# Attention and expert layer on one core: denominators transposed out of PSUM by VectorE, and the maxima's transfers issued by SyncE

## The chip, the cores and the metric

The kernel runs on one core of one Trainium2 chip. The time is device microseconds of that core, from runs without the profiler. A separate, profiled execution gave the trace that is read here. Of the engines, TensorE (PE in the rows, PEld for its weight loads) multiplies matrices, VectorE is DVE, ScalarE is ACT, GpSimd is POOL, and SyncE (SP) only issues transfers. "ACTq" and "SPq" are the instruction queues of ScalarE and SyncE, where issues of transfers stand.

## The reference

Pooled attention, then a layer with a squared ReLU, all in float32. There are 4 batches of 8 heads, 1152 keys and 576 pooled queries per head, 64 columns per head; the second layer has 2304 tokens, 512 model columns and 2048 hidden columns.

```python
q_pool = q.reshape(B, H, S // 2, 2, D).mean(axis=3)
scores = scale * np.matmul(q_pool, k.transpose(0, 1, 3, 2))
scores = scores - np.max(scores, axis=-1, keepdims=True)
attn = np.exp(scores)
attn = attn / (np.sum(attn, axis=-1, keepdims=True) + 1e-09)
x = np.matmul(attn, v)            # heads side by side: 2304 x 512
h = x @ w_in
g = s * np.maximum(h, 0.0) ** 2 + b
out = g @ w_out
```

## The kernel before

The attention stage goes through 32 heads, two heads to a pair, in one long loop of steps: nine steps to a head, one for each tile of 128 keys. In step n the kernel multiplies the scores of key tile j of one head into a PSUM tile `s_j` (keys on partitions, queries in two halves of 288 columns, `score_step`, line 486), ScalarE takes their exponential, and three steps later the products of the exponentials with v are added up (`value_step`, lines 518 to 528) in two PSUM tiles `o_0` and `o_1`, one for each half of the queries. Numbers are split into a high and a low part for accuracy: `ph` is the exponential rounded, `pl` the rest, which VectorE or GpSimd computes; one kind of step (`w`) keeps a full `pe` and has no `pl`. There are two `s` buffers. A step's exponentials must be read out before its buffer takes the scores of a later step.

The values have 64 columns, and 64 columns of ones stand beside them. So partitions 0 to 63 of `o` hold the sums of the products and partitions 64 to 127 hold the softmax's denominator, 64 times the same row. When the last product of a head is in, `finish` empties both `o` tiles: ScalarE copies each into `xu` (products) and into `l` (denominators, with 1e-9 added), four copies in all. The next head's first products wait until they are done. When both heads of a pair are there, VectorE transposes `l` in 32x32 blocks into `lt`, takes the reciprocal of one column of each block, and transposes that back over the block; GpSimd multiplies, and SyncE stores the result to DRAM. These steps are put off by the number of ticks in `XT`; one tick is one step of the loop.

The maximum of the scores is subtracted inside the score matmul. A head's maxima are found ahead of its turn, over 27 "units" to a pair: a matmul `m` (line 456) of the same scores with queries on partitions, and a VectorE reduce `pm` (457). After the last unit of a head a short reduce gives `c` (468), 128 partitions by 5 numbers, and two small transfers (471, 472) lay them out as row 64 of `qq`, the moving operand of the score matmul. So the first scores of a head need that head's `c` to have landed. Before the loop 15 steps' worth of units run, which gives the first head its `c`.

Beside this, each pair's keys and queries are loaded two or three pairs ahead (`kraw`, `qraw`; 350, 358), transposed by VectorE (`kT`, `qT`; 411, 413, 415), split, and laid out by transfers into `kk` and `qq` (404 to 407). `qm` is a 64x64 corner of `qT` which ScalarE copies (212).

Every engine and every queue works in the order in which the code issues. There is no scheduler: ticks, `ORD`, `PP`, `PREP` and `XT` fix the order. An instruction that has to wait holds back all that stand behind it on its engine, and an issue of a transfer that has to wait holds back the queue.

When all heads are through, the second layer runs over nine blocks of 256 tokens in three sweeps over the hidden columns. None of the edited lines belongs to it.

Of the kernel before, what the change touches and what calls it, by code (L numbers as in the profile page):

```python
# [8 lines left out]
F32 = mybir.dt.float32  # L9
# [3 lines left out]
AF = mybir.ActivationFunctionType  # L13
ALU = mybir.AluOpType
# [27 lines left out]
XT = (1, 2, 3, 4, 8)  # L42
# [10 lines left out]
def f32(ap):  # L53
    return ap.bitcast(F32)
# [3 lines left out]
def attention_moe_kernel(ctx: ExitStack, tc: tile.TileContext, q, k, v, w_in, w_out, s_in, b_in, out):  # L58
    nc = tc.nc
    B, H, S, D = q.shape  # L60
    SQ = S // 2
    HALF = SQ // 2
    NT, DM = out.shape
    DFF = w_in.shape[1]
    P = 128
    NJ = S // P
    NB = S // 32
    NBQ = SQ // 32
    NT4 = SQ // P
# [6 lines left out]
    EPS = 1e-9  # L76
# [7 lines left out]
    ep = ctx.enter_context(tc.tile_pool(name="ep", bufs=1))  # L84
# [136 lines left out]
    def later(k, fn):  # L221
        step[1] += 1
        queue.append((step[0] + k, step[1], fn))
# [238 lines left out]
    def shift(hd, pm, full, rest):  # L462


        c = ap.tile([P, NT4 + 1], F32R, tag="c", bufs=2, name=f"c{hd}")
        row = qqs[hd % 3][:, 1].rearrange("p a n -> p (a n)")
        h = hd % 2
        nc.vector.tensor_reduce(out=c, in_=pm, axis=AX.X, op=ALU.max)

        def send():  # L470
            nc.scalar.dma_start(f32(row[D:D + 1, :NT4 * P]), f32(c[:, full]))
            nc.scalar.dma_start(f32(row[D:D + 1, NT4 * P:]), f32(c[h * D:(h + 1) * D, rest:rest + 1]))
            holds["c", hd % 3] = hd

        later(1, send)
# [28 lines left out]
    xu = {}  # L504
    inv = {}
    xs = {}

    def value_step(hd, j):
        assert holds["v", hd % 2] == hd
        vv, vl = vvs[hd % 2], vls[hd % 2]  # L510
        ph, pl = prob.pop((hd, j))
        if j == 0:
            acc[hd] = [ps_o.tile([P, 512], F32, tag=f"o{a}", name=f"o{hd}_{a}") for a in range(2)]
        first, last = j == 0, j == NJ - 1
        for a in range(2):
            o = acc[hd][a]
            if pl is None:
                nc.tensor.matmul(o[:, :HALF], vfs[hd % 2][:, j], ph[:, a], start=first, stop=last)  # L518
                if a == 1 and last:
                    finish(hd)  # L520
                for _ in range(3):
                    yield
                continue
            nc.tensor.matmul(o[:, :HALF], vv[:, j], ph[:, a], start=first, stop=False)  # L524
            yield
            nc.tensor.matmul(o[0:D, :HALF], vl[:, j], ph[:, a], start=False, stop=False)  # L526
            yield
            nc.tensor.matmul(o[:, :HALF], vv[:, j], pl[:, a], start=False, stop=last)  # L528
            if a == 1 and last:
                finish(hd)  # L530
            yield

    def finish(hd):
        o = acc.pop(hd)
        p, h = divmod(hd, 2)
        if h == 0:
            xu[p] = (
                ep.tile([P, 2, HALF], F32, tag="xu", name=f"xu{p}"),
                ep.tile([P, 2, HALF], F32, tag="l", name=f"l{p}"),
            )  # L540
        x, l = xu[p]
        r = slice(h * D, (h + 1) * D)
        for a in range(2):
            nc.scalar.activation(x[r, a], o[a][0:D, :HALF], AF.Copy)  # L544
            nc.scalar.activation(l[r, a], o[a][D:P, :HALF], AF.Copy, bias=EPS)  # L545

        def invert():
            lt = ep.tile([P, NBQ, 32], F32, tag="lt", name=f"lt{p}")
            nc.vector.transpose(out=lt, in_=l.rearrange("p a n -> p (a n)"))
            inv[p] = lt  # L550

        def reciprocal():
            lt = inv[p]
            rc = inv[p] = ep.tile([P, NBQ, 1], F32, tag="rc", name=f"rc{p}")
            nc.vector.reciprocal(rc, lt[:, :, 0:1])

        def spread():
            rc = inv[p]
            inv[p] = ep.tile([P, NBQ, 32], F32, tag="lt", name=f"rr{p}")
            nc.vector.transpose(out=inv[p], in_=rc.to_broadcast([P, NBQ, 32]))  # L560

        def scale():
            xo = xs[p] = ep.tile([P, SQ], F32, tag="xo", name=f"xo{p}")
            nc.gpsimd.tensor_tensor(out=xo, in0=x.rearrange("p a n -> p (a n)"), in1=inv.pop(p).rearrange("p j c -> p (j c)"), op=ALU.mult)

        def send():
            nc.sync.dma_start(xd[hd // H][(hd % H) // 2], xs.pop(p))

        if h == 1:
            for at, fn in zip(XT, (invert, reciprocal, spread, scale, send)):  # L570
                later(at, fn)

    load_k(0)
# [47 lines left out]
    for n in range(NS + LAG):  # L621
        hd, j = divmod(n, NJ)

        at = (n - LAG) % NJ if n >= LAG else None
# [16 lines left out]
        if n < NS:  # L641
            p, h = divmod(hd, 2)
# [59 lines left out]
    for m in range(len(work) + DEPTH):  # L702
        if m < len(work):
            i, blk, f, fs = work[m]
# [10 lines left out]
        if m >= DEPTH:  # L715
            _, blk, f, fs = work[m - DEPTH]
# [35 lines left out]
```

## Time and profile before

| | us |
|---|---|
| median of 3 runs | 961.16 (958.78 to 962.41) |
| span of the profiled execution | 960.4 |
| attention stage, to the first matmul of the second layer | 541.9 |
| TensorE busy | 915.8 (95% of the span) |
| VectorE busy | 621.5 (65%) |
| ScalarE busy | 546.4 (57%) |
| GpSimd busy | 507.0 (53%) |

The page gives a span for the profiled execution, from its first to its last instruction, and no other time; the runs without the profiler lie around it. A busy share is an average over stages. A matmul that is late shows as idle time of TensorE before it, with the releaser in square brackets at the end of a row. Starts are in us from the start of the span; the second number of a timeline row is how long the instruction took, in us, and "x2" that two neighbours are shown together.

### The profile page before, as it was taken

How to read it: one execution, taken by the hardware profiler on the slowest of the kernel's cores; microseconds unless marked ns; L12 is line 12 of the kernel's file. 1: busy time of each engine (PE TensorE's matmuls, PEld its weight loads, DVE VectorE, ACT ScalarE, POOL GpSimd, SP SyncE). 2: the span in 40 equal slices, each digit the busy share in tenths (PEclk: the TensorE clock that was granted, in tenths of full speed). 3: DMA queues.
4: the chain of work that ended last, by engine and by line, in shares of the span. 5: the costliest groups of instructions: out<-in, count | busy, mean ns of one | idle time of the engine just before them, and what ended most of it. 6: DMA issues, size and time to landing. Idle time of an engine off the chain costs nothing.

```text
span 960.4 us, 16166 instructions
## 1 busy us (share of the span) xinstructions
PE 915.8 (95%) x5712; PEld 818.2 (85%) x5712; DVE 621.5 (65%) x1168; ACT 546.4 (57%) x1054; POOL 507.0 (53%) x405
## 2 busy tenths in 40 slices
PE   5899999999999999999999989999999999999998
PEld 3788888888888888888888879889999899999997
DVE  5767777777767777877766366767667653334333
ACT  2766666666666676777767656554444433333332
POOL 7567656765676577678756476763453520201000
PEclk9999999999999999999999999999999999999999
DMA  8978776867686778787762245555444432223211
GB/s 151 169 145 171 150 151 122 175 149 148 130 165 145 156 144 187 159 162 147 191 149 69 66 156 187 181 197 163 140 143 165 132 111 67 67 88 107 70 45 44
DMA packets 255312, 131.17 MB, mean 137 GB/s; under 512 B 203776, under 2 KB 227328, under 8 KB 255232
## 3 DMA queue, kind: packets, MB, share of 16 engines
q1 hardware_dynamic: 244512, 129.62, 56.2%
q10 hardware_dynamic: 10720, 0.52, 0.7%
q8 instruction: 46, 0.75, 0.3%
q14 instruction: 34, 0.28, 0.1%
HBM read 68.68 MB, written 18.87 MB: 91 GB/s over the span
## 4 chain that ended last, share of the span: by engine, by line
PE 72%; ACT 13%; DVE 4%; DMA 3%; issue 2%; POOL 2%; ACTq 1%; SPq 0%; POOLq 0%; DVEq 0%
PE h L272 18%; PE y L299 17%; PE s L486 14%; PE o L518 6%; PE m L456 5%; PE o L524 4%; PE o L526 4%; PE o L528 4%; ACT ph L495 4%; ACT xu L544 2%; ACT s L498 2%; ACT l L545 2%; DMA xr<-xd 2%; DVE pm L457 1%; ACT pe L498 1%
## 5 line engine op out<-in xcount | busy, mean ns | idle before, releaser
L457 DVE TENSOR_REDUCE pm<-m 128x1 f32<-128x384 f32 x432 | 230.8, 550 | 98.4 <-PE m L456 92.2
L486 PE MATMUL s<-qq,kk 128*128 128x288 f32 x1152 | 215.6, 309 | 10.6 <-ACT pe L498 6.3
L272 PE MATMUL h<-x,wih 128*128 128x256 f32 x1152 | 213.9, 283 | 6.8 <-DVE gl L286 5.7
L272 PEld LDWEIGHTS h<-x,wih 128*128 128x128 f32 x1152 | 186.8, 189 | 20.9 <-DVE gl L286 6.7
L495 ACT ACTIVATE ph<-s 128x576 fp32r<-128x576 f32 x192 | 125.3, 653 | 130.5 <-PE s L486 108.1
L486 PEld LDWEIGHTS s<-qq,kk 128*128 128x128 f32 x1152 | 173.5, 190 | 26.2 <-ACT pe L498 9.0
L272 PE MATMUL h<-x,wil 128*128 128x256 f32 x576 | 162.8, 283 | 0.0
L501 POOL TENSOR_TENSOR pl<-pe,ph 128x576 fp32r<-128x576 f32 x64 | 91.1, 1424 | 125.7 <-ACT pe L498 115.7
L456 PE MATMUL m<-kh,qz 128*128 128x384 f32 x384 | 155.6, 414 | 1.4 <-DVE pm L457 1.4
L280 DVE SCALAR_TENSOR_TENSOR h<-h,sb,r 128x256 f32<-128x256 f32 x144 | 70.3, 488 | 114.7 <-ACT r L289 114.7
L253 POOL TENSOR_TENSOR x<-xr,x 128x1024 fp32r<-128x1024 f32 x27 | 64.9, 2402 | 148.8 <-ACT x L212 143.1
L524 PE MATMUL o<-ph,vv 128*128 128x288 f32 x384 | 119.1, 310 | 9.0 <-issue 5.3
L518 PE MATMUL o<-pe,vf 128*128 128x288 f32 x384 | 123.2, 405 | 0.0
L501 DVE TENSOR_TENSOR pl<-s,ph 128x576 fp32r<-128x576 f32 x128 | 96.4, 753 | 37.6 <-ACT s L498 32.6
L289 ACT ACTIVATE r<-h 128x256 f32<-128x256 f32 x144 | 55.8, 387 | 112.1 <-PE h L272 112.1
L526 PE MATMUL o<-ph,vl 128*64 128x288 f32 x384 | 113.3, 295 | 0.0
L299 PE MATMUL y<-wol,gh 128*128 128x512 f32 x288 | 113.3, 393 | 0.0
L299 PE MATMUL y<-woh,gl 128*128 128x512 f32 x288 | 113.0, 392 | 0.0
L299 PE MATMUL y<-woh,gh 128*128 128x512 f32 x288 | 112.9, 392 | 0.0
L528 PE MATMUL o<-pl,vv 128*128 128x288 f32 x384 | 112.8, 294 | 0.0
L272 PEld LDWEIGHTS h<-x,wil 128*128 128x128 f32 x576 | 110.1, 191 | 0.0
L283 ACT ACTIVATE gh<-h,sb 128x256 fp32r<-128x256 f32 x144 | 68.3, 474 | 64.4 <-DVE h L280 64.1
(89 smaller groups left out, 1500.5 us busy)
## 6 DMA issues: line engine op xcount, KB each, us to landing
kk<-kh SPq DMA_DIRECT2D x32, 576.0 KB, 6.0
kraw<-in_k_dram SPq DMA_DIRECT2D x64, 144.0 KB, 3.5
vf<-in_v_dram SPq DMA_DIRECT2D x32, 288.0 KB, 4.4
kk<-kT SPq DMA_DIRECT2D x32, 288.0 KB, 4.9
qq<-qh SPq DMA_DIRECT2D x64, 144.0 KB, 6.0
xr<-xd SPq DMA_DIRECT2D x18, 512.0 KB, 3.9
qraw<-in_q_dram SPq DMA_DIRECT2D x122, 72.0 KB, 2.6
wsti<-in_moe_w_in_dram SPq DMA_DIRECT2D x16, 512.0 KB, 4.7
```

Of the source, the lines that this page charges most:

```text
L272: nc.tensor.matmul(h[:, :TB], st[:, c, :], mv[:, c, :], start=(n == 0), stop=(n == 3 * NC - 1))
L280: nc.vector.scalar_tensor_tensor(out=t, in0=h[:, :TB], scalar=sb[:, 0:1], in1=r, op0=ALU.mult, op1=ALU.mult)
L299: nc.tensor.matmul(y[:, :DM], st[:, ts_], mv, start=(first and n == 0), stop=(last and n == 2))
L456: nc.tensor.matmul(ps[:, :KB], st, khs[p][:, e * KB:(e + 1) * KB], start=True, stop=True)
L457: nc.vector.tensor_reduce(out=pms[p][:, col, e:e + 1], in_=ps[:, :KB], axis=AX.X, op=ALU.max)
L486: nc.tensor.matmul(ps[:, a, :HALF], kk[:, i, j * P:(j + 1) * P], qq[:, i, a], start=(i == 0), stop=(i == 1))
L495: nc.scalar.activation(ph, ps[:, :, :HALF], AF.Exp, scale=SCALE)
L501: fresh.append(lambda: eng.tensor_tensor(out=pl, in0=full, in1=f32(ph), op=ALU.subtract))
L518: nc.tensor.matmul(o[:, :HALF], vfs[hd % 2][:, j], ph[:, a], start=first, stop=last)
L524: nc.tensor.matmul(o[:, :HALF], vv[:, j], ph[:, a], start=first, stop=False)
L526: nc.tensor.matmul(o[0:D, :HALF], vl[:, j], ph[:, a], start=False, stop=False)
L528: nc.tensor.matmul(o[:, :HALF], vv[:, j], pl[:, a], start=False, stop=last)
```

## The change

Two things change. In `finish`, ScalarE keeps the copy of the products, and VectorE transposes the denominators out of PSUM straight into `lt`, one 64x288 transpose for each `o` tile and head. The 1e-9 is added afterwards to the one column of each block that is used (`guard`), the reciprocal is taken in place, and the spread result has a buffer of its own. In `shift`, the two small transfers of `c` are issued by SyncE instead of ScalarE.

```diff
         def send():
-            nc.scalar.dma_start(f32(row[D:D + 1, :NT4 * P]), f32(c[:, full]))
-            nc.scalar.dma_start(f32(row[D:D + 1, NT4 * P:]), f32(c[h * D:(h + 1) * D, rest:rest + 1]))
+            nc.sync.dma_start(f32(row[D:D + 1, :NT4 * P]), f32(c[:, full]))
+            nc.sync.dma_start(f32(row[D:D + 1, NT4 * P:]), f32(c[h * D:(h + 1) * D, rest:rest + 1]))
@@ finish
-                ep.tile([P, 2, HALF], F32, tag="l", name=f"l{p}"),
+                ep.tile([P, NBQ, 32], F32, tag="lt", name=f"lt{p}"),
...
             nc.scalar.activation(x[r, a], o[a][0:D, :HALF], AF.Copy)
-            nc.scalar.activation(l[r, a], o[a][D:P, :HALF], AF.Copy, bias=EPS)
-
-        def invert():
-            lt = ep.tile([P, NBQ, 32], F32, tag="lt", name=f"lt{p}")
-            nc.vector.transpose(out=lt, in_=l.rearrange("p a n -> p (a n)"))
-            inv[p] = lt
+            nc.vector.transpose(out=lt[r].rearrange("p j c -> p (j c)")[:, a * HALF:(a + 1) * HALF], in_=o[a][D:P, :HALF])
+
+        def guard():
+            rc = inv[p] = ep.tile([P, NBQ, 1], F32, tag="rc", name=f"rc{p}")
+            nc.vector.tensor_scalar(out=rc, in0=lt[:, :, 0:1], scalar1=1.0, scalar2=EPS, op0=ALU.mult, op1=ALU.add)
 
         def reciprocal():
-            lt = inv[p]
-            rc = inv[p] = ep.tile([P, NBQ, 1], F32, tag="rc", name=f"rc{p}")
-            nc.vector.reciprocal(rc, lt[:, :, 0:1])
+            nc.vector.reciprocal(inv[p], inv[p])
 
         def spread():
             rc = inv[p]
-            inv[p] = ep.tile([P, NBQ, 32], F32, tag="lt", name=f"rr{p}")
+            inv[p] = ep.tile([P, NBQ, 32], F32, tag="rr", name=f"rr{p}")
```

VectorE's order at the end of head 8, the first of pair 4, before. `pl_2` belongs to step 2 of the next head, `kT` and `qT` to the preparation of a later pair:

```order
L457 TENSOR_REDUCE pm_1988<-m_12_2162 128x1
L501 TENSOR_TENSOR pl_2_2158<-s_2_2152,ph_2_2157 128x576
L413 STREAM_TRANSPOSE kT_2125<-kraw_1842 128x576
L457 TENSOR_REDUCE pm_1988<-m_13_2185 128x1
L457 TENSOR_REDUCE pm_1988<-m_14_2191 128x1
L468 TENSOR_REDUCE c_2194<-pm_1988 128x5
L415 STREAM_TRANSPOSE qT_2126<-qs_2127 128x576
```

And the same place now:

```order
L457 TENSOR_REDUCE pm_1985<-m_12_2158 128x1
L545 STREAM_TRANSPOSE lt_2163<-o_0_1989 64x288
L545 STREAM_TRANSPOSE lt_2163<-o_1_1990 64x288
L501 TENSOR_TENSOR pl_2_2154<-s_2_2148,ph_2_2153 128x576
L413 STREAM_TRANSPOSE kT_2121<-kraw_1839 128x576
L457 TENSOR_REDUCE pm_1985<-m_13_2181 128x1
L457 TENSOR_REDUCE pm_1985<-m_14_2187 128x1
L468 TENSOR_REDUCE c_2190<-pm_1985 128x5
L415 STREAM_TRANSPOSE qT_2122<-qs_2123 128x576
```

The two transposes stand between the reduce and `pl_2`, and `c` and `qT` come after them. Each of the two waits for ScalarE's copy of the same `o` tile.

ScalarE's order at the same place, before:

```order
L544 ACTIVATE xu_2166<-o_0_1992 64x288
L545 ACTIVATE l_2167<-o_0_1992 64x288
L544 ACTIVATE xu_2166<-o_1_1993 64x288
L545 ACTIVATE l_2167<-o_1_1993 64x288
L495 ACTIVATE ph_3_2181<-s_3_2175 128x576
L498 ACTIVATE pe_3_2180<-s_3_2175 128x576
L471 DMA qq_98<-c_2194 1x128x4
L472 DMA qq_98<-c_2194 1x64x1
L495 ACTIVATE ph_4_2213<-s_4_2208 128x576
L498 ACTIVATE s_4_2208<-s_4_2208 128x2x288
L212 ACTIVATE qm<-qT_2126 64x64 x2
L490 ACTIVATE pe_5_2238<-s_5_2233 128x576
```

And now:

```order
L544 ACTIVATE xu_2162<-o_0_1989 64x288
L544 ACTIVATE xu_2162<-o_1_1990 64x288
L495 ACTIVATE ph_3_2177<-s_3_2171 128x576
L498 ACTIVATE pe_3_2176<-s_3_2171 128x576
L495 ACTIVATE ph_4_2209<-s_4_2204 128x576
L498 ACTIVATE s_4_2204<-s_4_2204 128x2x288
L212 ACTIVATE qm<-qT_2122 64x64 x2
L490 ACTIVATE pe_5_2234<-s_5_2229 128x576
```

Two copies and two issues are gone; `qm` still stands in front of `pe_5`.

SyncE's order at the start of the program now; `c_232` holds the maxima of head 0, and `kk_95`, `qq_98` are the operands of head 1:

```order
L358 DMA qraw_160<-in_q_dram 32x18x32 x8
L404 DMA kk_95<-kT_132 64x1152
L404 DMA kk_95<-kh_135 64x2x1152
L405 DMA qq_98<-qh_136 64x576
L406 DMA qq_98<-qh_136 64x576
L407 DMA qq_98<-qT_133 64x576
L471 DMA qq_97<-c_232 1x128x4
L472 DMA qq_97<-c_232 1x64x1
L363 DMA vf_104<-in_v_dram 128x9x64
```

Before, the two `c_232` rows were not on this queue; they stood on ScalarE, behind the preparation of pair 0 and in front of the first exponential. The other rows are as they were.

## Rows read from the trace of the kernel before

**Rows 1.** The page: the chain that ended last, by engine.
```profile
PE 72%; ACT 13%; DVE 4%; DMA 3%; issue 2%; POOL 2%; ACTq 1%; SPq 0%; POOLq 0%; DVEq 0%
```

**Rows 2.** Windows: length, then busy us of PE, PEld, DVE, ACT, POOL; clock; DMA.
```profile
200.00:300.00 100.00, 96.72 (x610) 86.72 (x609) 72.65 (x133) 67.38 (x124) 66.02 (x54) 1.00 0.75 151
```

**Rows 3.** Waits, 60 to 500 us: total us, times, longest.
```profile
PE s L486 <- ACT pe L498: 5.0, 9, 0.6
```

**Rows 4.** Timeline of ScalarE, end of head 8: start, took, instruction, idle before.
```profile
174.90 0.41 ACT L545 ACTIVATE l<-o 64x288 f32<-64x288 f32 x1
...
176.19 0.65 ACT L495 ACTIVATE ph<-s 128x576 fp32r<-128x576 f32 x1
...
177.78 0.80 ACTq L472 DMA_DIRECT2D qq<-c  x1
178.63 0.65 ACT L495 ACTIVATE ph<-s 128x576 fp32r<-128x576 f32 x1 [1.25 <-PE s L486]
...
179.85 0.53 ACT L212 ACTIVATE qm<-qT 64x64 fp32r<-64x64 f32 x2
180.40 0.66 ACT L490 ACTIVATE pe<-s 128x576 f32<-128x576 f32 x1
```

**Rows 5.** Timeline of VectorE, the same place.
```profile
174.61 0.76 DVE L501 TENSOR_TENSOR pl<-s,ph 128x576 fp32r<-128x576 f32 x1
...
176.99 0.17 DVE L468 TENSOR_REDUCE c<-pm 128x5 fp32r<-128x15 f32 x1
177.08 0.77 DVE L415 STREAM_TRANSPOSE qT<-qs 128x576 f32<-128x576 f32 x1
```

**Rows 6.** Timeline of TensorE: scores of steps 4, 6, and the next head's first.
```profile
177.43 0.80 PE L486 MATMUL s<-qq,kk 128*128 128x288 f32 x4 [0.56 <-ACT pe L498]
...
180.87 0.69 PE L486 MATMUL s<-qq,kk 128*128 128x288 f32 x4
...
185.50 0.91 PE L486 MATMUL s<-qq,kk 128*128 128x288 f32 x4
```

**Rows 7.** Groups by line, VectorE: busy us, mean ns | idle before, releaser.
```profile
L457 DVE TENSOR_REDUCE pm<-m 128x1 f32<-128x384 f32 x432 | 230.8, 550 | 98.4 <-PE m L456 92.2
...
L549 DVE STREAM_TRANSPOSE lt<-l 128x576 f32<-128x576 f32 x16 | 12.4, 774 | 7.2 <-ACT l L545 7.2
...
L555 DVE RECIPROCAL rc<-lt 128x18 f32<-128x18 f32 x16 | 4.0, 247 | 0.1
```

**Rows 8.** Timeline after an odd head, number 17: ScalarE's `ph_3`, step 4's scores.
```profile
321.65 0.66 ACT L495 ACTIVATE ph<-s 128x576 fp32r<-128x576 f32 x1 [0.41 <-issue]
...
321.79 0.69 PE L486 MATMUL s<-qq,kk 128*128 128x288 f32 x4
```

**Rows 9.** Timeline of SyncE's queue at the start.
```profile
18.80 6.45 SPq L358 DMA_DIRECT2D qraw<-in_q_dram  x8
...
29.89 0.92 SPq L407 DMA_DIRECT2D qq<-qT  x1
```

**Rows 10.** Timeline at the start: the second c transfer, and the first scores.
```profile
20.32 0.60 ACTq L472 DMA_DIRECT2D qq<-c  x1
...
22.02 1.33 PE L486 MATMUL s<-qq,kk 128*128 128x288 f32 x4 [0.24 <-DVE pm L457]
```

**Rows 11.** Transfers (KB each, us to landing) and SyncE's waits, at the start.
```profile
qq<-c ACTq DMA_DIRECT2D x1, 0.2 KB, 1.8
...
sb<-in_moe_s_dram SPq DMA_DIRECT2D x1, 0.5 KB, 3.8
...
SPq L358 <- DMA qq<-c: 2.3, 1, 2.3
```

**Rows 12.** Timeline after head 28: a long issue, and scores that wait.
```profile
500.93 2.65 ACTq L472 DMA_DIRECT2D qq<-c  x1
...
505.44 0.79 PE L486 MATMUL s<-qq,kk 128*128 128x288 f32 x4 [1.61 <-ACT pe L490]
```

**Rows 13.** Windows in the second layer's start; the clock is the third from last.
```profile
574.00:575.00 1.00, 1.00 (x6) 1.00 (x6) 0.90 (x2) 0.00 (x0) 1.00 (x1) 0.50 0.00 0
```

More of the change, by code (lines that the diff above doesn't have):

```diff
@@ L538, in finish @@
                 ep.tile([P, 2, HALF], F32, tag="xu", name=f"xu{p}"),
-                ep.tile([P, 2, HALF], F32, tag="l", name=f"l{p}"),
+                ep.tile([P, NBQ, 32], F32, tag="lt", name=f"lt{p}"),
             )
-        x, l = xu[p]
+        x, lt = xu[p]
         r = slice(h * D, (h + 1) * D)
@@ L569, in finish @@
         if h == 1:
-            for at, fn in zip(XT, (invert, reciprocal, spread, scale, send)):
+            for at, fn in zip(XT, (guard, reciprocal, spread, scale, send)):
                 later(at, fn)
```

## The prediction

> **What bounds the kernel now.** The chain that ended last is 72% TensorE and 13% ScalarE [rows 1], so I read the attention stage, which holds every edited line, by windows first. From 200 to 300 us TensorE is busy 96.7 of 100 us, VectorE 72.7 and ScalarE 67.4, with the granted clock at 1.00 [rows 2]: time is to be had only where TensorE stands still. The MoE stage runs no edited line after its first microseconds, so only its start time can move.
>
> The table of waits names the place. Between 60 and 500 us score matmuls wait for ScalarE's `pe` exponential, 5.0 us in 9 waits [rows 3]. The timeline around one of them, 174 us, shows why: a head has just finished, ScalarE copies its two accumulators out in four copies, and the exponentials of the next step stand behind them [rows 4]. I call a head with an even number boundary A, one with an odd number boundary B. There are 16 of each. At A the chain is xu, l, xu, l, then `ph_3` at 176.19, `pe_3` behind it, then the score matmuls of step 4 at 177.43, which name `pe` as what they waited for [rows 4, 6]. The two `qq<-c` issues follow on ScalarE's queue until 178.58 and hold back `ph_4`, which starts after 1.25 us of idleness [rows 4]. At B the step-4 scores start at 321.79 and wait for no `pe` [rows 8].
>
> **The change, part by part.**
>
> *ScalarE at A.* Each head loses two l copies. The first l starts at 174.90 where the second xu can now start, the second xu takes about as long as an l, 0.41, and 0.04 is the gap behind it [rows 4]: `ph_3` starts at 175.35 instead of 176.19, so 0.84 us earlier. `pe_3` follows it as before, and step 4 starts at 176.59 instead of 177.43, if nothing else is late. The next accumulators are no obstacle: they wait for two VectorE transposes, priced next, that end at 175.43 and 175.90, and TensorE has the max matmuls and three products of the first accumulator between.
>
> *VectorE at A.* Two 64x288 transposes out of PSUM are added, for which the trace has no row. The 128x576 transpose from SBUF takes 774 ns, that is 0.17 beside 1 column per 1.04 ns; the PSUM reduce over 384 columns takes 550 ns, 0.15 beside the same rate [rows 7]. So I take 300 + 175 = 0.475 us for 288 columns. From below, 0.17 us (the same fixed part and hidden columns) and from above 0.77 us (the whole 576-column transpose [rows 7]) bound it. In the order each transpose stands behind ScalarE's xu of the same accumulator. VectorE is free when `pl_2` began, at 174.61 [rows 5], and the first xu ends at about 174.90, so the first transpose runs from 174.95 to 175.43, the second to 175.90. Behind them in VectorE's order stand `pl_2` itself, a `kT` transpose, two reduces, c and the `qT` transpose that ended at 177.85 [rows 5]. All keep their 3.24 us and slide by 1.29: `qT` ends at 179.14.
>
> What is late next is ScalarE's `qm`, which reads `qT`: 179.18 to 179.71 (0.53), then `pe_5` (0.66) until 180.39 [rows 4]. The scores of step 6 now wait for `pe_5` (their buffer has changed), so they start at 180.45. Before, they started at 180.87 [rows 6]. So of 0.84 gained, 0.42 remains at A: 16 x 0.42 = 6.7 us.
>
> [...]
>
> *The issues leave ScalarE.* At a usual A they delay `ph_4` by about 1 us, and that is already inside the 0.42, since `ph_4` is no longer the limit. Where an issue is slow it costs more: at 500.93 one took 2.65 us and the scores at 505.44 waited 1.61 us for it [rows 12]. That wait goes: 1.6 us. So A gains 6.7 + 1.6 = 8.3 us.
>
> *At B* the second reduce and `pl_2` move behind the transposes, and step 4 now waits for `pe_3`. From A's spacing (175.35 to 176.59 for `ph_3` to step 4) and B's `ph_3`, which at 321.65 stood behind two copies and 0.41 us of issuing and can now start at about 320.4, step 4 starts at about 321.7, against 321.79 [rows 8]: nothing, between a gain of 0.1 and a loss of 0.3 per B. The 16 guards, the reciprocals in place and the shorter transposes run in VectorE's idle time, which is 27% of the stage [rows 2]. They hide there; uncovered they cost 16 x 0.25 = 4 us at most (the price of a reciprocal [rows 7]). The later multiply and store have no reader before the MoE.
>
> *The transfers on SyncE's queue.* In the middle of the stage there is room. At A, c slides with `qT`, from 176.99 to 178.28 [rows 5]; with issues of about 0.6 us the second starts at 179.0, and 3.8 us later (the landing used below) it is there, at 182.8. The next head's first scores start at 185.50, or 0.42 earlier [rows 6]. At the start there is none. The first maxima were issued by ScalarE at 20.32 (the second of two transfers) and landed 1.8 us later, at 22.1; the first scores began at 22.02, and their last of four matmuls, about 0.72 us later, needed them [rows 10, 11]. In the new order the two transfers stand on SyncE behind eight `qraw` loads and the five `kk` and `qq` transfers of head 1, which SyncE issued from 18.80 to 30.81 [rows 9]. One wait in that run goes away, the 2.3 us for c itself [rows 11], so the run ends at 28.5. The two issues start at 28.5 and 29.1. A half-kilobyte transfer on SyncE's queue at 31.75 took 3.8 us to land [rows 11], so c is there at 32.9 instead of being in time for a matmul at 22.74. The start is 10.2 us later; 0.3 us of waiting for a `qraw` load behind it goes. Cost: 9.9 us. Bounds: 8.2 with the landing of 1.8 us, 12.5 if the 2.3 us remain. Nothing hides it, as every engine's program passes through the first scores. The pause may lower the granted clock: in the second layer it stood at 0.50 between 574 and 575 [rows 13], shortly after a pause. At half speed three such microseconds would cost an estimated 1.5 us more; I add nothing, since the first four score matmuls took 1.33 us before as well [rows 10], against 0.69 later [rows 6].
>
> **The sum.** 960.4 + 9.9 - 8.3 = 962.0 us of span. The median of the runs, 961.16, is 0.8 above the profiled span; so 962.8, call it 963.
>
> **The rivals.** *ScalarE's relief is kept whole.* If the transposes are near the lower bound and `qT` is not late, 0.84 remains at each A: 16 x 0.84 + 1.6 = 15.0 us, so 960.4 + 9.9 - 15.0 + 0.8 = 956 us. For it speaks that ScalarE's chain is what ends the wait now [rows 3]; against it, that VectorE has no pause in its order between 174 and 177.9 [rows 5].
>
> *The first maxima are not late*, because SyncE gets through its earlier transfers sooner: 960.4 - 8.3 + 0.8 = 953 us. Against it: the order, and the five issues behind the loads, which alone took 5.5 us, from 25.25 to 30.81 [rows 9].
>
> *Slower: VectorE's order gives everything back.* Its place is A, `pl_2` to `qT` to `qm` to `pe_5`. It decides from the point where VectorE's slide is 1.29 + 0.42 = 1.71 us, that is with transposes of about 0.69 us each. Then the steady gain is nothing: 960.4 + 9.9 + 0.8 = 971 us. For it: 0.69 lies inside my bound of 0.77. Against: both nearest rows give 0.475.
>
> *Slower: SyncE's queue makes c late at later heads too*, since it holds waits of its own; 1 us late at 16 heads gives 963 + 16 = 979 us. The change does do what it says: the order shows both moves.
>
> **How the numbers follow.** The forecast has 0.56, with 958 to 968 of its own; relief kept whole 0.14, no late start 0.06, VectorE gives back 0.17, later heads late 0.07. The range from 955 to 970 takes in the first two and the better part of the fourth. A difference under 0.5%, 4.8 us, cannot be told from no change here. Faster: 0.06 and 0.08 of the second case, 0.14. Slower: 0.17, 0.07 and 0.04 of the forecast's upper end, 0.28. Same: 0.58.
>
> **What would show it.** Right: the first `ph` at about 33.5 us instead of 23.4; transposes near 0.475 us; at A, step 4 waiting for `pe_3` some 0.8 us earlier, step 6 waiting for `pe_5`, about 0.4 us earlier; the MoE starting 1 to 2 us later than at 541.9. Wrong: c landed before 25 us; `qT` done before 178.5 in its place; waits of first scores for `qq<-c` at later heads.

## The result, and the profile after

The changed kernel takes 966.55 us (median of four runs, 965.36 to 967.24), beside 961.11 for the kernel before: ratio 1.0053, 95% interval 1.0035 to 1.0072. That lies in the range, 3.6 us above the forecast. The prediction took a difference under 0.5% as no change; this one, 0.53%, lies at that line. The profiled execution has a span of 965.5 us, 5.0 more than before.

The best single view is the start of every step's first score matmul, in both traces. The differences of neighbouring starts, summed by place, say where the time went (us; minus is faster). Pairs count from 0; B of pair n is the boundary at which pair n begins, so [rows 8] shows B of pair 9, and A of pair n lies between its two heads:

| | forecast | measured |
|---|---|---|
| start, to step 8 of the first head | +9.9 | +10.3 |
| A, sixteen times | -8.3 | -9.3 |
| B of pairs 1 to 9 | 0 | +1.1 |
| B of pairs 10 to 15 | 0 | +5.5 |
| elsewhere in the attention stage | 0 | -0.2 |
| attention stage | +1.6 | +7.4 |
| MoE | 0 | -2.4 |
| span | +1.6 | +5.0 |

*The start.* SyncE's issues (start, duration, queue, line; the last two are c) and TensorE's first scores:

```profile
18.72 4.62 SPq L358 DMA_DIRECT2D qraw<-in_q_dram  x8
...
28.19 0.82 SPq L407 DMA_DIRECT2D qq<-qT  x1
29.11 0.54 SPq L471 DMA_DIRECT2D qq<-c  x1
29.70 0.65 SPq L472 DMA_DIRECT2D qq<-c  x1
```

```profile
22.28 0.61 PE L486 MATMUL s<-qq,kk 128*128 128x288 f32 x1 [0.24 <-DVE pm L457]
31.82 1.06 PE L486 MATMUL s<-qq,kk 128*128 128x288 f32 x3 [8.94 <-issue]
```

The first of four matmuls ran on time. The second needs c (row 64 of `qq`, in the code), and it and the two behind it came 8.94 us later; the prediction had only the last of the four need it. The releaser is printed as "issue", which here hides a landing: the row of the queue names it, the second issue at 29.70 with 2.2 us to its landing. [rows 10] showed the four together in 1.33 us.

*A, the end of head 8, the place of [rows 4 to 6].* ScalarE, VectorE, and the scores of steps 4, 5 and 6:

```profile
182.89 0.68 ACT L544 ACTIVATE xu<-o 64x288 f32<-64x288 f32 x2
183.46 0.64 ACT L495 ACTIVATE ph<-s 128x576 fp32r<-128x576 f32 x1
184.00 0.65 ACT L498 ACTIVATE pe<-s 128x576 f32<-128x576 f32 x1
185.72 0.65 ACT L495 ACTIVATE ph<-s 128x576 fp32r<-128x576 f32 x1 [1.08 <-PE s L486]
...
187.51 0.52 ACT L212 ACTIVATE qm<-qT 64x64 fp32r<-64x64 f32 x2 [0.60 <-DVE qT L415]
188.06 0.66 ACT L490 ACTIVATE pe<-s 128x576 f32<-128x576 f32 x1
```

```profile
183.31 0.86 DVE L545 STREAM_TRANSPOSE lt<-o 64x288 f32<-64x288 f32 x2 [0.32 <-ACT xu L544]
184.20 0.76 DVE L501 TENSOR_TENSOR pl<-s,ph 128x576 fp32r<-128x576 f32 x1
184.88 0.77 DVE L413 STREAM_TRANSPOSE kT<-kraw 128x576 f32<-128x576 f32 x1
...
186.59 0.17 DVE L468 TENSOR_REDUCE c<-pm 128x5 fp32r<-128x15 f32 x1
186.70 0.78 DVE L415 STREAM_TRANSPOSE qT<-qs 128x576 f32<-128x576 f32 x1
```

```profile
185.00 0.69 PE L486 MATMUL s<-qq,kk 128*128 128x288 f32 x4
186.69 0.92 PE L486 MATMUL s<-qq,kk 128*128 128x288 f32 x4
188.77 0.80 PE L486 MATMUL s<-qq,kk 128*128 128x288 f32 x4
```

From step 3, step 4 comes 0.83 us earlier than before, step 5 0.69, step 6 0.50, step 7 0.40. Not every A is like this one, as is told further down. The end of the give-back is readable: `qm` waits 0.60 us for `qT`, `pe` follows, and the next scores start 0.05 us after it.

*B, which was to cost nothing.* At pair 9, [rows 8] of before; VectorE, GpSimd and TensorE:

```profile
327.79 0.75 DVE L501 TENSOR_TENSOR pl<-s,ph 128x576 fp32r<-128x576 f32 x1
328.46 0.78 DVE L549 TENSOR_SCALAR rc<-lt 128x18 f32<-128x18 f32 x1
329.15 0.55 DVE L457 TENSOR_REDUCE pm<-m 128x1 f32<-128x384 f32 x1
```

```profile
327.78 1.42 POOL L501 TENSOR_TENSOR pl<-pe,ph 128x576 fp32r<-128x576 f32 x1 [3.31 <-ACT pe L498]
```

```profile
327.75 0.81 PE L486 MATMUL s<-qq,kk 128*128 128x288 f32 x4
...
329.75 0.44 PE L456 MATMUL m<-kh,qm 128*128 128x384 f32 x1
330.03 0.69 PE L486 MATMUL s<-qq,kk 128*128 128x288 f32 x4
```

The guard works on 18 numbers per partition and takes 0.78 us. It ends at 329.24, GpSimd's `pl` at 329.20. The reduce behind it is late, so the max matmul (its buffer) and the scores are late: step 4 to 5 takes 2.28 us instead of 1.85. Before, step 4 began at 321.79 [rows 8] and step 5 here:

```profile
323.64 0.69 PE L486 MATMUL s<-qq,kk 128*128 128x288 f32 x4
```

The whole line of the guard (count, shortest, median, longest in ns):

```profile
L549 DVE TENSOR_SCALAR rc<-lt x16: 164/774/1409, 74.5 to 550.7; 128x18 f32<-128x18 f32 x16
```

From pair 10 on the conversion of the second layer's weights stands there as well. Pair 11:

```profile
392.82 1.65 DVE L161 TENSOR_SCALAR wabo<-whmo 128x512 int32<-128x512 int32 x1
394.38 0.16 DVE L549 TENSOR_SCALAR rc<-lt 128x18 f32<-128x18 f32 x1
```

```profile
392.77 1.41 POOL L501 TENSOR_TENSOR pl<-pe,ph 128x576 fp32r<-128x576 f32 x1
```

```profile
395.07 0.45 PE L456 MATMUL m<-kh,qm 128*128 128x384 f32 x1 [1.02 <-DVE pm L457]
```

Here `wab` is caught instead, 1.65 us, and the guard behind it runs free in 0.16. In pairs 12 to 14 `wab` gets in first (0.42) and the guard is caught for 1.38. Before, the line of `wab` took this (two tiles, `wi` and `wo`):

```profile
L161 DVE TENSOR_SCALAR wabi<-whmi x3: 416/786/860, 353.4 to 483.1; 128x512 int32<-128x512 int32 x3
L161 DVE TENSOR_SCALAR wabo<-whmo x3: 821/842/2323, 385.8 to 517.0; 128x512 int32<-128x512 int32 x3
```

So one instruction with durations of 0.42, of 0.79 to 0.86 and of 2.32 us stood in the trace of before: the sign that something else decides how long it lasts.

*The MoE* lasts 416.1 us instead of 418.5. The difference opens at one place. Before, TensorE waits 1.80 us for VectorE's `gl` there, and the stretch at half clock of [rows 13] follows (0.50); after, the same wait is 0.44 and no such stretch follows (the clock is 1.00 from 577.4 to 587.4):

```profile
573.13 0.61 PE L272 MATMUL h<-x,wih 128*128 128x256 f32 x2 [1.80 <-DVE gl L286]
```

```profile
579.47 0.51 PE L272 MATMUL h<-x,wih 128*128 128x256 f32 x2 [0.44 <-DVE gl L286]
```

About 1.4 us are the shorter wait and another 1.4 the full clock of the matmuls behind it; 0.4 came back elsewhere. In the traces of the experiments the MoE lasts 415.8 to 417.3. That the change shortened the wait is not shown: with the transfers alone from the third head on it is 2.41 us, and no half clock follows it (the mean granted clock of that profiled run is 1.000).

### The profile page after: what moved, and what is told of

Read it like the earlier page. It is cut to its first block, busy times and chain, and to the rows that moved or that the text cites. A ratio compares the mean times of both kernels' runs of the same rounds, so it can differ in the third digit from the quotient of the medians.

```text
span 965.5 us, 16055 instructions
## 1 busy us (share of the span) xinstructions
PE 916.7 (95%) x5712; PEld 816.3 (85%) x5712; DVE 646.9 (67%) x1232; ACT 517.1 (54%) x990; POOL 507.8 (53%) x405
## 4 chain that ended last, share of the span: by engine, by line
PE 73%; DVE 10%; ACT 7%; DMA 4%; issue 2%; POOL 1%; SPq 1%; ACTq 0%; POOLq 0%; DVEq 0%
PE h L272 18%; PE y L299 17%; PE s L486 13%; PE m L456 6%; PE o L518 5%; PE o L524 5%; PE o L526 5%; PE o L528 5%; DVE pm L457 2%; ACT ph L495 2%; DVE lt L545 2%; ACT s L498 2%; DMA wsto<-in_moe_w_out_dram 2%; DVE pl L501 1%; ACT xu L544 1%
## 5 line engine op out<-in xcount | busy, mean ns | idle before, releaser
L524 PE MATMUL o<-ph,vv 128*128 128x288 f32 x384 | 116.1, 302 | 10.8 <-DVE lt L545 10.8
```

## The experiments

The kernel before was timed again beside each group of experiments, with medians of 960.07 to 961.11 us, so medians of different groups compare to about 1 us. The ratios are to the kernel before in the same group.

**The transposes alone.**

```diff
-            nc.sync.dma_start(f32(row[D:D + 1, :NT4 * P]), f32(c[:, full]))
+            nc.scalar.dma_start(f32(row[D:D + 1, :NT4 * P]), f32(c[:, full]))
```

(and the second transfer likewise)

> The change without its second half: VectorE transposes the denominators, but c still leaves on ScalarE's queue. Theory (the halves are coupled: the two transposes put c about 1 to 2 us later on VectorE, and the issues of c stand on ScalarE in front of ph_3 at B and of ph_4 at A): the start is as before, no 10 us; at each B ph_3 starts some 1.9 us later and step 4, which now waits for pe_3, about 3 us; at each A step 6 is about 1.3 us later than before. 960 + 16 x (3.0 + 1.3) = about 1030 us. Rival (the start's delay is all that separates the change from its gain, and c's issue hides): 966.5 - 10.3 = about 956 us.

989.23 us, ratio 1.0312 (1.0291 to 1.0333). ScalarE at A:

```profile
182.90 0.65 ACT L498 ACTIVATE pe<-s 128x576 f32<-128x576 f32 x1
185.69 0.49 ACTq L471 DMA_DIRECT2D qq<-c  x1
186.28 0.56 ACTq L472 DMA_DIRECT2D qq<-c  x1
186.88 0.65 ACT L495 ACTIVATE ph<-s 128x576 fp32r<-128x576 f32 x1 [3.34 <-PE m L456]
```

The issue waits for c, which VectorE now has later, and the next `ph` stands behind it for 3.34 us. The start is as before; against before most A's lose 0.6 to 1.1 us and most B's 0.8 to 1.3. The coupling is shown; I had priced B three times too high. One thing more shows in this run. The guard stands at the same place, right behind `pl_2`, and takes 0.17 us at B of every pair from 1 to 15, where the changed kernel has 0.77 to 1.41 in most; its longest is at the end of the last head. GpSimd's `pl` of B of pair 9, held back with ScalarE's `pe`, starts only after it:

```profile
L549 DVE TENSOR_SCALAR rc<-lt x16: 165/168/509, 66.0 to 572.1; 128x18 f32<-128x18 f32 x16
```

```profile
337.82 0.17 DVE L549 TENSOR_SCALAR rc<-lt 128x18 f32<-128x18 f32 x1
```

```profile
340.12 1.44 POOL L501 TENSOR_TENSOR pl<-pe,ph 128x576 fp32r<-128x576 f32 x1 [7.66 <-ACT pe L498]
```

**The transfers alone**, in the kernel before.

> The change without its first half: the l copies stay on ScalarE, c leaves on SyncE's queue. Theory: the start costs the same 10.3 us as in the changed kernel; at A TensorE already ran without a pause from step 4 to step 7, so only the A's with a slow issue gain, 1.6 to 5 us in all: 961.1 + 10.3 - (1.6 to 5) = 966 to 970 us. Rival (SyncE's queue costs nothing or the extra time of the changed kernel comes from the transposes): 958 to 961 us.

964.18 us, ratio 1.0044 (1.0030 to 1.0058), just under what was expected. The start costs +9.8. But A of pairs 0 to 9 gains 0.83 or more with all four copies still on ScalarE, which neither theory had, and step 1 to 2 of 14 pairs loses 0.70 (one of them 0.56). The scores of step 4 and ScalarE's `pe` of step 3:

```profile
185.22 0.56 PE L486 MATMUL s<-qq,kk 128*128 128x288 f32 x3
```

```profile
185.23 0.65 ACT L498 ACTIVATE pe<-s 128x576 f32<-128x576 f32 x1
```

Step 4 starts while `pe_3` has just begun: it uses the other `s` buffer. In this kernel's code step 4 at A waits for VectorE's `pl_2`; in the kernel before it waits for ScalarE at A of pairs 0 to 9, and for `pl_2` from pair 10 on. Most of what is gained there (14.8 us at A) is lost at pair starts (9.6), where products now wait for GpSimd's `pl` (6.1 us in 14 waits).

**Only the first head's c from ScalarE**, in the changed kernel.

```diff
-            nc.sync.dma_start(f32(row[D:D + 1, :NT4 * P]), f32(c[:, full]))
+            eng = nc.scalar if hd == 0 else nc.sync
+            eng.dma_start(f32(row[D:D + 1, :NT4 * P]), f32(c[:, full]))
```

(and the second transfer likewise)

> The changed kernel, but the very first head's c is issued by ScalarE as before, all 31 others by SyncE. Theory (the start's cost is the first head's c behind SyncE's loads, once): the first three score matmuls no longer pause 8.9 us, first ph near 23.5, 966.5 - 10 = about 956.5 us. Rival (a later c or the pause's after-effects carry part of it): 960 to 963 us.

962.79 us, ratio to the kernel before 1.0028 (1.0017 to 1.0039): the rival. SyncE, and the second head's first scores (lines from 471 on stand one further down in this kernel):

```profile
32.97 3.65 SPq L350 DMA_DIRECT2D kraw<-in_k_dram  x4
36.72 5.11 SPq L358 DMA_DIRECT2D qraw<-in_q_dram  x8
41.94 0.53 SPq L472 DMA_DIRECT2D qq<-c  x1
```

```profile
44.03 0.72 PE L487 MATMUL s<-qq,kk 128*128 128x288 f32 x3 [3.54 <-DMA qq<-c]
```

Ten microseconds earlier, the second head needs its c while SyncE is still issuing twelve loads: 5.4 us come back there. In the changed kernel the late start had hidden this.

**The first two heads' c from ScalarE** (`hd < 2` in the line above).

> The changed kernel, the c of the first two heads issued by ScalarE, the other 30 by SyncE. Theory (with only the first there, the second head's c stood behind the twelve key and query loads on SyncE, 3.5 us of waiting and two slow steps, 5.4 us in all; with both there the whole start cost is back): 966.5 - 10.3 = about 956.5 us. Rival (the third head's c is late in its turn, or ScalarE is held by the second c): 959 to 963 us.

957.00 us, ratio 0.9954 (0.9941 to 0.9967). The first head is 10.4 us shorter and nothing else differs by 0.1 us.

**No guard.** 1e-9 is left out.

```diff
-            nc.vector.tensor_scalar(out=rc, in0=lt[:, :, 0:1], scalar1=1.0, scalar2=EPS, op0=ALU.mult, op1=ALU.add)
...
-            nc.vector.reciprocal(inv[p], inv[p])
+            nc.vector.reciprocal(rc, lt[:, :, 0:1])
```

> The changed kernel without the guard: 1e-9 is left out, the reciprocal reads the transposed column directly. Theory (the guard, 18 elements per partition, is held until GpSimd's pl ends, 0.77 to 1.4 us instead of 0.16, and holds up a reduce and with it a max matmul at B): step 4 to 5 at B back from 2.28 to about 1.85 us in pairs 1 to 9, about 1.2 us back in each of pairs 12 to 14, pairs 10 and 11 little, since there another VectorE operation is held; in all 4 + 4 = 8 us: about 958.5 us. Rival (B's loss comes from the reduces having slid behind the transposes, and the guard is 0.16 us each): -1.6 us at most, 965 us.

961.15 us, 5.4 below the changed kernel. B of pairs 1 to 9 gains 0.33 each, B of pairs 11 and 15 1.2 to 1.3 each, and pairs 12 to 14 only 0.1, against an expected 1.2, since now `wab` is caught there. VectorE and GpSimd of pair 12:

```profile
420.97 1.64 DVE L161 TENSOR_SCALAR wabi<-whmi 128x512 int32<-128x512 int32 x1
```

```profile
420.92 1.40 POOL L501 TENSOR_TENSOR pl<-pe,ph 128x576 fp32r<-128x576 f32 x1
```

**The guard as another kind of instruction**, same place, same operands; 1e-9 is left out.

```diff
-            nc.vector.tensor_scalar(out=rc, in0=lt[:, :, 0:1], scalar1=1.0, scalar2=EPS, op0=ALU.mult, op1=ALU.add)
+            nc.vector.tensor_reduce(out=rc, in_=lt[:, :, 0:1], axis=AX.X, op=ALU.max)
```

> The changed kernel, the guard at its old place, but as a reduce over one element (1e-9 is left out; same input, output and 18 elements per partition) instead of a multiply-add. Theory (this form of instruction, reading and writing SBUF, is what GpSimd's pl holds; a reduce is not held): it lasts about 0.2 us, step 4 to 5 at B about 1.95 us, the same time as without a guard: 961 to 962 us. Rival (whatever stands there is held, by a semaphore or by its place): 0.77 us again in pairs 0 to 8, 965 to 967 us.

961.54 us, as without a guard. The line now:

```profile
L549 DVE TENSOR_REDUCE rc<-lt x16: 170/173/185, 73.8 to 544.6; 128x18 f32<-128x18 f32 x16
```

It runs in 0.17 us right beside GpSimd's `pl`. So it was neither a semaphore nor the place, but the kind of instruction, at a time when `pl` runs.

**The guard directly behind the transposes.**

```diff
         if h == 1:
-            for at, fn in zip(XT, (guard, reciprocal, spread, scale, send)):
+            guard()
+            for at, fn in zip(XT[1:], (reciprocal, spread, scale, send)):
```

> The changed kernel, the guard issued directly behind the two transposes of an odd head instead of one tick later. Theory (the guard was held by GpSimd's pl; earlier, GpSimd works on nothing that holds it): the guard takes 0.16 us in pairs 0 to 9, step 4 to 5 at B falls from 2.28 to about 1.95 us, the saving is that of leaving the guard out less up to 0.1 us a head: 966.5 - 5.4 + (0 to 1.6) = 961 to 962.7 us. Rival (the cost is that of one more VectorE instruction at B, wherever it stands): 965 to 967 us.

963.59 us, 3.0 below the changed kernel and 0.9 above the end of what was expected:

```profile
L549 DVE TENSOR_SCALAR rc<-lt x16: 176/179/2171, 72.0 to 546.6; 128x18 f32<-128x18 f32 x16
```

The guard is free now, but `wab` is caught for 1.43 us in pairs 11 to 14 in its stead, and in pair 15 the guard lasts 2.17 us beside a 2.4 us GpSimd operation.

**`qm` behind `pe_5`.**

```diff
-PREP = (..., ("qm", 13), ...)
+PREP = (..., ("qm", 14), ...)
```

> The changed kernel, qm issued one tick later, behind pe_5 instead of in front of it. Theory (at A VectorE's later qT holds qm and so pe_5 and the scores of step 6): step 5 to 6 at A falls from 2.07 to about 1.88 us and step 6 to 7 from 1.60 to 1.50, 0.2 to 0.3 us at 14 heads: 962.5 to 964 us. Rival (step 6 waits for something else): 966 to 967 us.

963.17 us. Step 5 to 6 at A falls by 0.15 to 0.20 and step 6 to 7 by 0.10, at 14 heads. That `qm`, late with `qT`, takes back part of the gain at A is shown.

**All together.** Besides three edits from above (the first two c from ScalarE, the early guard, `qm` behind `pe_5`), `wab` of the weight conversion comes two ticks later, at the tick of `wA`, which takes 0.68 us there in the changed kernel.

```diff
-STA = (0, 1, 3, 5, 7, 18, 19, 20)
+STA = (0, 1, 5, 5, 7, 18, 19, 20)
```

> All three at once, and besides the two steps of the weight conversion that stand on VectorE at B of pairs 10 to 15 (wab and wA) one after the other at the later of their ticks, when GpSimd has nothing that holds them. Theory (the savings add up, and the held conversion cost about 1.1 us in four to five pairs): 966.5 - 10 - 5 - 3 - 4.5 = about 944 us. Rival (each stall gone uncovers the next one, half is kept): 953 to 956 us.

948.70 us, ratio 0.9864 (0.9848 to 0.9880): faster than both kernels. Against the changed kernel the first head gives 10.1 us, B of pairs 1 to 9 0.3 each, B of pairs 10 to 14 3.1 in all, A 0.3 each at 14 heads. Three things kept it from 944: VectorE has both conversion steps at one place (+0.5 us at step 6 to 7 of five pairs), pair 15's guard is caught again (2.17 us), and the MoE lasts 1.0 us longer, for which no cause is shown.

**`wA` one tick later** (`STA = (0, 1, 5, 6, ...)`).

> The combined kernel with wA one tick behind wab instead of together with it. Theory (in pairs 10 to 14 both at one place made VectorE late by 0.5 us at step 6 to 7): 5 x 0.5 = 2.5 us less, 946.2 us. Rival (wA then meets GpSimd's xo and is held): 948.7 us or more.

950.71 us: the rival. `wA`, 1.69 us here and 0.68 in the changed kernel, and the GpSimd operation beside it:

```profile
413.72 1.69 DVE L164 SCALAR_TENSOR_TENSOR wAi<-wsti,wabi 128x512 int32<-128x512 int32 x1
```

```profile
413.43 1.42 POOL L562 TENSOR_TENSOR xo<-xu,rr 128x576 f32<-128x576 f32 x1 [2.13 <-DVE rr L558]
```

**The transfers alone, from the third head on**, in the kernel before.

> The kernel before, with c on SyncE's queue from the third head on, the first two heads' c by ScalarE as before; nothing else changed. Theory (the start cost comes off whole, as it did with the transposes): 964.2 - 9.9 = about 954.3 us, which is less than the 957.0 us of the same with the transposes, so the transposes as changed cost 2.7 us. Rival (the gain at the ends of heads comes from the transposes and ScalarE's two copies): 958 to 961 us.

954.32 us, ratio 0.9928 (0.9910 to 0.9946). With the same start the transposes make it 957.00: as changed, they cost 2.7 us in the medians and 1.9 in the attention stage of the two traces. There each A of pairs 1 to 13 is 0.4 us longer with them and each B of pairs 11 to 15 0.4 to 0.5; B of pairs 2 to 9 is 0.6 shorter, since the wait for GpSimd's `pl` at step 1 to 2 is gone. Whether the transposes pay once the guard and `wab` are out of `pl`'s way is not shown: no run has the kernel of this experiment with `wab` moved.

## Why the prediction was right, and where it was not

*The total: near, in part by luck.* B cost 6.6 us that were priced at nothing. A came out 1.0 better than forecast and the MoE 2.4 shorter, which took half of that back. A sign that was named for being right failed: the MoE was to start 1 to 2 us later than at 541.9 and starts 7.4 us later, at 549.3.

*ScalarE at A: right in place, the size by luck.* 0.84 us earlier was forecast for step 4, 0.83 measured at head 8. But ScalarE gave more than that: `ph_3` starts 0.96 us after the first score matmul of step 3 (182.50) instead of 2.08, so 1.12 earlier, and `pe_3` is done at 184.65. And the next accumulators, "no obstacle" in the prediction, are one. The first product waits for the first transpose, and the products behind it run until 185.0, where step 4 starts:

```profile
183.94 0.37 PE L524 MATMUL o<-ph,vv 128*128 128x288 f32 x1 [0.35 <-DVE lt L545]
```

Nor are the sixteen A's alike. The wait for `pe` stood at A of pairs 0 to 9 alone ([rows 3] counts nine), and only there step 4 is 0.83 to 0.85 earlier. From pair 10 on step 4 of the kernel before waits for `pl_2`; it is 0.10 to 0.29 earlier now, and A of pairs 10 to 13 and 15 gains about 0.3 each. That `pe_3` bounds step 4 at all comes from which `s` buffer step 4 gets; the transfers alone changed that too.

*VectorE at A: right.* A transpose lasts 0.484 us (median; 0.475 assumed). `qT` slides as forecast, and of 0.84 us 0.39 to 0.41 remains at A of pairs 2, 3, 4 and 6 (0.42). The rate in the 0.475, 1.04 ns a column, is near what two rows of the trace before give: the reduces over 384 and over 15 columns take 550 and 170 ns [rows 7, 5], 1.03 ns for each column more. At head 8 `pl` starts 0.03 us after the transposes' end, and `kT` 0.08 before the end of `pl`: about 0.1 us less overlap behind the transposes.

*Slow issues: right in kind.* Pair 14's A gains 2.1 us, of which 1.6 was forecast for the late scores; pairs 0, 1, 8 and 9 gain 0.7 instead of 0.4, where smaller waits for the issues went too (the transfers alone give these four 0.2 to 0.3 at step 5 to 6).

*The start: right, with two errors that nearly cancel.* +10.3 for 9.9. The issues came 0.6 us later than worked out, at 29.11 and 29.70, but the second landed 2.2 us after its issue instead of 3.8, a price that came from a load out of DRAM. So c was there 1.0 us sooner, and step 1 is 9.5 us late. The other 0.8 came up to step 8, where TensorE's matmuls stay slow longer, for which the prediction added nothing. The bounds of 8.2 and 12.5 leave out the 0.3 us that the 9.9 counts. A product still takes 0.44 us at 40.70 and 0.30 from 44.91, where before it took 0.29 from 30.03 (the column of the granted clock prints 1.00 in both stretches, so the durations are the sign):

```profile
40.70 0.44 PE L528 MATMUL o<-pl,vv 128*128 128x288 f32 x1
...
44.91 0.30 PE L524 MATMUL o<-ph,vv 128*128 128x288 f32 x1
```

*B: wrong, and it is the miss.* The failed step is that the guards and the rest "run in VectorE's idle time", with 16 x 0.25 = 4 us as the most they could cost, and B between -0.1 and +0.3. An idle share says nothing of an instruction that is held, and the price was taken from a reciprocal, another kind of instruction. In the runs: the guard is held until GpSimd's `pl` ends (0.77 us at B of pairs 1 to 9), or the conversion is, for up to 1.65 us. Both hits have one cause, the new meeting of VectorE's and GpSimd's work: at B `pl_2` and what follows come later behind the transposes, and ScalarE's relief lets GpSimd's `pl` start earlier. It takes both halves: with the transposes alone, c's issues hold ScalarE's `pe` and so `pl` back, and the guard is free, as is `wab` at pairs 10 to 14 (0.42). From pair 10 on either instruction can be the one that is caught: with the first two c from ScalarE, the guard is caught at pairs 11 and 12 and `wab` at 13 and 14, and the time is the same to 0.1 us a pair. B cost 6.6 us, 4.1 of it as the excess over 0.13 each in pairs 10 to 14.

Beside GpSimd's `pl` or `xo` the guard, `wab` and `wA` took 0.78, 1.65 and 1.69 us; where nothing held them, 0.17, 0.42 and 0.68. Not every VectorE instruction is held: the guard as a reduce took 0.17 us beside `pl`, and all 64 transposes from PSUM took 0.445 to 0.488 us, also the two of 390.58, which ran beside a TENSOR_TENSOR of GpSimd's (390.17, 1.27 us). What sets the guard, `wab` and `wA` apart from these no run here shows.

*Rivals.* ScalarE's relief was not kept whole: `qT` is late. The first maxima were late. VectorE did not give A back. No c is late at later heads, though it was close: without the late start the second head's would be.

The forecast for the MoE, that its start alone moves, took the wait and the half-clock stretch of one trace as given. The mean granted clock of that execution is 0.998. It is 1.000 in those of the changed kernel, the transposes alone, the guard as a reduce, all together and the transfers alone from the third head on: none of these has such a stretch. The times do not show a lower clock: of the 56 runs of the kernel before beside the experiments, 15 have a mean granted clock of 1.000, and their median is 960.7 us, against 960.8 for the rest.

## What to carry to other kernels

Before costing a small VectorE instruction at nothing, look up what GpSimd does at that moment, and look for the same form of instruction with several durations in the trace: here that spread, 0.16 to 1.41 us for the guard, was the price of meeting GpSimd. Count at how many places a wait stands before multiplying by all of them. When work moves to another queue, read what stands in that queue at the first use and at the second; a late start can hide the next late transfer (here 3.54 us of waiting). Take the halves of a change apart on the chip (1.031 and 1.004 alone, 1.005 together, 0.993 for the transfers alone from the third head on, 0.986 with both halves and the repairs).

## What was not expected of the hardware

An instruction over 18 numbers per partition took 2.17 us (the guard of pair 15, issued early). The hold goes both ways: GpSimd's `pl`, 1.42 us in the median, takes 1.69 us at 426.05, where `wab` got in first. And, not of the chip but of the program: moving two transfers to another queue changed which `s` buffer the scores of step 4 get, in a place with no edited line, worth 0.83 us at one end of a head and -0.70 at the next pair's start.
